# The last expert's contraction in two token passes in an attention, MLP and routed-expert kernel

## The chip, the cores and the metric

The kernel runs on one core of one Trainium2 chip, in one launch. The metric is device time in microseconds (us). The core has five engines: TensorE (PE, with its weight loads shown apart as PEld), VectorE (DVE), ScalarE (ACT), GpSimd (POOL) and SyncE (SP). Each has its own queue of instructions, and they meet through semaphores.

## What is computed

Three stages follow one another: attention over a window of 128 keys, a dense MLP, and eight experts to which 2304 tokens are routed, 288 to each. The change lies in the last stage alone, whose core is this (the routing, which fills `assigned`, is left out):

```python
def _moe2_ref(x, w_gate, w1, w2):
    N, D = x.shape                 # 2304, 512
    E = w_gate.shape[1]            # 8
    cap = N // E                   # 288
...
    out = np.zeros((N, D), dtype=np.float32)
    for e in range(E):
        mask = assigned == e
        h = np.maximum(x[mask] @ w1[e], 0.0)
        out[mask] = h @ w2[e]
    return out.astype(np.float32)
```

`w1` is 512 x 1024 for each expert and `w2` is 1024 x 512. Every product of two float32 numbers is made of three products of the reduced type fp32r: both operands are split into a high part (`wh`, `hh`) and a low part (`wl`, `hl`), and wh x hh, wl x hh and wh x hl are summed in PSUM.

## The kernel before

In the expert stage all engines run in the order in which the code is written (`manual_schedule`), so the order around the change is the order of the Python loops from L1041 on.

For each expert, `expand_expert(e, f)` (L975) makes one of eight blocks of 128 hidden features for all 288 tokens: 12 matmuls, a relu on ACT into `hh`, the low part on DVE into `hl`. Then `contract_expert(e, d)` (L995) makes one of four blocks of 128 output features: 24 matmuls (8 hidden blocks f, three products each) into the PSUM bank `y`. The stationary operand of each is a 128 x 128 piece of `w2` (`wh_w` or `wl_w`), and the moving operand is `hh` or `hl`, 128 x 288. Consecutive matmuls have different stationary operands, so each has its weight load of 128 columns. ACT then copies the bank to `yt[:, d, :]` (L1008). The banks with the tag `s` are two.

The results are feature-major and have to be written as rows of tokens. `output_transpose(e, g, d)` (L1012) transposes one block of 128 features by 96 tokens (g is one of three groups of 96 tokens, GR in the code) on PE into the bank `yo`; its moving operand is a 128 x 128 identity and its stationary one a 128 x 96 piece of `yt`. `output(e, g)` (L1017) copies the four blocks to `ys` (on ACT or on DVE) and lets POOL scatter its 96 rows to their places in the output by an indirect DMA (L1025), behind a tiny memset (L1024).

For experts 0 to 6 the transposes and outputs stand between the expansions of the expert after. For the last one nothing follows: three transposes, one of each group, stand behind each of the output blocks 1, 2 and 3 (they are those of the block before), and the three transposes of block 3 and all three outputs stand behind the last matmul (L1055 to L1060).

Of the kernel before, what the change touches and what calls it, by code (L numbers as in the profile page):

```python
# [14 lines left out]
AF = mybir.ActivationFunctionType  # L15
# [9 lines left out]
NE = 8  # L25
CAP = N // NE
# [47 lines left out]
G = 3  # L74
GR = CAP // G
# [51 lines left out]
def tile_attn_moe_moe2(ctx: ExitStack, tc: tile.TileContext, q_in, k_in, v, w_in, w_out, w_gate, w1, w2, consts, out):  # L127
    nc = tc.nc
    V, A, T, GP = nc.vector, nc.scalar, nc.tensor, nc.gpsimd
# [9 lines left out]
    def bank(tag, name, bufs=None):  # L139
        kw = {} if bufs is None else dict(bufs=bufs)  # L140
        return ps.tile([P, 512], F32, tag=tag, name=name, **kw)
# [109 lines left out]
    def gather(e):  # L251
        for g in range(G):
            xg[e, g] = xpool.tile([GR, DM], F32, tag="xg", name=f"xg_{e}_{g}", bufs=3)
            col = e * G + g
            src, at = (x2_dram[:, :], row) if e else (x2_dram[:N, :], idx)
            gathers[e, g] = GP.indirect_dma_start(
                out=xg[e, g], out_offset=None, in_=src,
                in_offset=bass.IndirectOffsetOnAxis(ap=at[:, col:col + 1], axis=0))
# [44 lines left out]
    with ExitStack() as actx:  # L303
# [279 lines left out]
        if True:  # L583
# [36 lines left out]
            s = 0  # L620
# [10 lines left out]
            while s <= max(NQ, late_end) or items or pending or tail:  # L631
# [5 lines left out]
                k = conv_at.get(s)  # L637
# [50 lines left out]
                for _ in range(2):  # L688
                    if s > gate_end and tail:
                        if staged and (len(tail) > 7 or len(items) <= len(tail)):  # L690
                            pool, lst, _, name = tail.pop(0)
# [257 lines left out]
    def gathered(e, g):  # L949
        if g == 0:  # L950
            expert_input(e)
        x = xg.pop((e, g))
        pt = bank("vlt"[g], f"xt_{e}_{g}", **({} if g == 2 else dict(bufs=1)))[:, :4 * GR].rearrange("p (d t) -> p d t", d=4)
        for d in range(4):
            T.transpose(pt[:, d, :], x[:, d * P:(d + 1) * P], ident[:GR, :GR])
        xh, xl = (t[:, :, g * GR:(g + 1) * GR] for t in xe[e])
        A.activation(xh, pt, AF.Copy)
        V.tensor_tensor(out=xl, in0=pt, in1=xh.bitcast(F32), op=ALU.subtract)
# [3 lines left out]
    def weights(n):  # L962

        nonlocal n_stage, n_split
        for _ in range(n):
            if n_split < 8 * NE:
                ready_w[n_split] = weight_tiles(ring[n_split % len(ring)](), f"w_{n_split}")
                split_weight(staged_w.pop(n_split), *ready_w[n_split], V)
                n_split += 1
            while n_stage < min(n_split + C_STAGES, 8 * NE):  # L970
                staged_w[n_stage] = stage(weight_src(n_stage), f"w_{n_stage}", epool,
                                          gathers[0, W_G] if n_stage == W_STAGED else None)
                n_stage += 1

    def expand_expert(e, f):  # L975
        if f == 0:
            hidden[e] = tuple(epool.tile([P, 8, CAP], F32R, tag=f"h{x}", name=f"h{x}_{e}", bufs=1)
                              for x in "hl")
        wh, wl = (t.rearrange("p (d f) -> p d f", d=4)[:, :, f % 2 * P:f % 2 * P + P]
                  for t in ready_w[8 * e + f // 2])  # L980
        (xh, xl), (hh, hl) = xe[e], hidden[e]
        hp = bank("h", f"m1_{e}_{f}")[:, :CAP]
        k = 0
        for w, x in ((wh, xh), (wl, xh), (wh, xl)):
            for d in range(4):
                T.matmul(hp, w[:, d, :], x[:, d, :], start=(k == 0), stop=(k == 11))  # L986
                k += 1
        A.activation(hh[:, f, :], hp, AF.Relu)
        V.scalar_tensor_tensor(out=hl[:, f, :], in0=hp, scalar=0.0, in1=hh[:, f, :].bitcast(F32),
                               op0=ALU.max, op1=ALU.subtract)  # L990
        weights(C_E0[f] if e == 0 else C_F[f])

    hidden, yt = {}, {}

    def contract_expert(e, d):  # L995
        if d == 0:
            yt[e] = epool.tile([P, 4, CAP], F32, tag="yt", name=f"yt_{e}", bufs=1)
        hh, hl = hidden[e]
        yp = bank("s", f"y_{e}_{d}")[:, :CAP]
        k = 0  # L1000
        for f in range(8):
            c = f % 2 * DM + d * P
            wh, wl = (t[:, c:c + P] for t in ready_w[8 * e + 4 + f // 2])
            for w, x in ((wh, hh), (wl, hh), (wh, hl)):
                T.matmul(yp, w, x[:, f, :], start=(k == 0), stop=(k == 23))  # L1005
                k += 1
        weights(1)
        A.activation(yt[e][:, d, :], yp, AF.Copy)  # L1008

    yo = {}  # L1010

    def output_transpose(e, g, d):  # L1012
        if d == 0:
            yo[g] = bank("ttv"[g], f"yo_{e}_{g}", **(dict(bufs=1) if g == 2 else {}))[:GR]
        T.transpose(yo[g][:, d * P:(d + 1) * P], yt[e][:, d, g * GR:(g + 1) * GR], ident)

    def output(e, g, on_act=True):  # L1017
        ys = epool.tile([GR, DM], F32, tag="ys", name=f"ys_{e}_{g}", bufs=3)
        if on_act:
            A.activation(ys, yo.pop(g), AF.Copy)  # L1020
        else:
            V.tensor_copy(ys, yo.pop(g))
        col = e * G + g
        GP.memset(spacer, 0.0)  # L1024
        sc = GP.indirect_dma_start(  # L1025
            out=out[:, :], out_offset=bass.IndirectOffsetOnAxis(ap=idx[:, col:col + 1], axis=0),
            in_=ys, in_offset=None)
        for other in scatters:
            tc.declare_no_dep(sc.ins, other.ins, reason="a token has one place")
        scatters.append(sc)  # L1030
# [10 lines left out]
    for e in range(NE):  # L1041
        for f in range(8):
            expand_expert(e, f)
            if f in (1, 2, 3) and e:
                for d in range(4):
                    output_transpose(e - 1, f - 1, d)
                output(e - 1, f - 1)
            if f == 4 and e + 1 < NE:
                gather(e + 1)
        for d in range(4):  # L1050
            contract_expert(e, d)
            if e + 1 < NE:
                if d < G:
                    gathered(e + 1, d)
            elif d:  # L1055
                for g in range(G):
                    output_transpose(e, g, d - 1)
    for g in range(G):
        output_transpose(NE - 1, g, 3)
        output(NE - 1, g, g != 1)  # L1060
    by_hand.close()


# [44 lines left out]
```

## Time and profile before

| | us |
|---|---|
| median of 3 runs | 915.43 |
| lowest and highest of them | 915.07 and 917.85 |
| the profiled execution, its own time | 917.14 |
| its span in the profile | 915.2 |

| engine | busy us | share of the span | instructions |
|---|---|---|---|
| PE | 841.4 | 92% | 7590 |
| PEld | 734.6 | 80% | 7590 |
| DVE | 521.9 | 57% | 1315 |
| ACT | 387.0 | 42% | 841 |
| POOL | 108.9 | 12% | 104 |

The profile is of one execution; its span is the time from its first to its last instruction. A matmul's duration in it is longer than its share of the engine's time, since matmuls are pipelined: what counts is the time from one start to the next, called a step below. A row that merges several instructions gives the time from the first's start to the last's end.

### The profile page before, as it was taken

How to read it: one execution, taken by the hardware profiler on the slowest of the kernel's cores; microseconds unless marked ns; L12 is line 12 of the kernel's file. 1: busy time of each engine (PE TensorE's matmuls, PEld its weight loads, DVE VectorE, ACT ScalarE, POOL GpSimd, SP SyncE). 2: the span in 40 equal slices, each digit the busy share in tenths (PEclk: the TensorE clock that was granted, in tenths of full speed). 3: DMA queues.
4: the chain of work that ended last, by engine and by line, in shares of the span. 5: the costliest groups of instructions: out<-in, count | busy, mean ns of one | idle time of the engine just before them, and what ended most of it. 6: DMA issues, size and time to landing. Idle time of an engine off the chain costs nothing.

```text
span 915.2 us, 18665 instructions
## 1 busy us (share of the span) xinstructions
PE 841.4 (92%) x7590; PEld 734.6 (80%) x7590; DVE 521.9 (57%) x1315; ACT 387.0 (42%) x841; POOL 108.9 (12%) x104
## 2 busy tenths in 40 slices
PE   2358698999999799999999999998999999999996
PEld 2347697999999688887677776776889999999995
DVE  3696856666654433247678777676235554555540
ACT  4454557566655544232212121211125555555551
POOL 1144411121110000000000000000020221122211
PEclk9998799999999899999999999998999999999998
DMA  9544666577546986585323324221425665676630
GB/s 275 158 157 141 217 179 190 159 226 235 163 127 171 286 227 159 147 246 148 141 93 107 119 77 133 85 98 52 130 104 187 191 183 168 190 226 201 187 122 27
DMA packets 103637, 147.19 MB, mean 161 GB/s; under 512 B 6144, under 2 KB 74368, under 8 KB 101504
## 3 DMA queue, kind: packets, MB, share of 16 engines
q1 hardware_dynamic: 100480, 136.56, 49.9%
q0 software_dynamic: 3072, 9.44, 3.1%
q8 instruction: 60, 0.98, 0.4%
q14 instruction: 25, 0.20, 0.1%
HBM read 113.21 MB, written 32.77 MB: 160 GB/s over the span
## 4 chain that ended last, share of the span: by engine, by line
PE 79%; DVE 9%; ACT 3%; issue 3%; DMA 3%; POOL 2%; SPq 0%; POOLq 0%; ACTq 0%; DVEq 0%
PE po L223 22%; PE h L505 20%; PE m L986 10%; PE y L1005 10%; PE xv L480 3%; PE cnt L806 3%; PE pt L463 2%; DMA raw<-in_w_in_dram 2%; PE lg L532 2%; PE s L421 2%; DVE dt L357 1%; DVE dt L356 1%; DVE dt L358 1%; PE wtp L384 1%; ACT pr L439 1%
## 5 line engine op out<-in xcount | busy, mean ns | idle before, releaser
L223 PE MATMUL po<-wh_out,gol 128*128 128x512 f32 x272 | 112.5, 414 | 4.7 <-DVE gol L191 4.6
L518 DVE TENSOR_TENSOR gb<-h,th 128x512 f32<-128x512 f32 x72 | 49.7, 691 | 109.1 <-ACT th L514 108.5
L223 PE MATMUL po<-wh_out,goh 128*128 128x512 f32 x272 | 110.9, 408 | 0.0
L223 PE MATMUL po<-wl_out,goh 128*128 128x512 f32 x272 | 110.6, 407 | 0.0
L505 PE MATMUL h<-xh,wh_in 128*128 128x256 f32 x576 | 96.0, 290 | 4.6 <-DVE gb L518 4.6
L505 PE MATMUL h<-xh,wl_in 128*128 128x256 f32 x576 | 91.9, 283 | 1.1 <-POOL wl_in L372 1.1
L505 PE MATMUL h<-xl,wh_in 128*128 128x256 f32 x576 | 90.9, 280 | 0.0
L183 ACT ACTIVATE goh<-gin 128x1024 fp32r<-128x1024 f32 x34 | 36.0, 1060 | 129.0 <-DMA gin<-g_dram 113.4
L160 DVE TENSOR_TENSOR wl_w<-st_w,wh_w 128x1024 fp32r<-128x1024 f32 x60 | 72.9, 1224 | 25.8 <-ACT wh_w L159 25.8
L505 PEld LDWEIGHTS h<-xh,wh_in 128*128 128x128 f32 x576 | 79.4, 194 | 9.7 <-DVE gb L518 4.8
L514 ACT ACTIVATE th<-h 128x512 f32<-128x512 f32 x72 | 42.7, 593 | 94.1 <-PE h L505 93.8
L505 PEld LDWEIGHTS h<-xh,wl_in 128*128 128x128 f32 x576 | 79.2, 194 | 1.3 <-POOL wl_in L372 1.3
L505 PEld LDWEIGHTS h<-xl,wh_in 128*128 128x128 f32 x576 | 78.3, 192 | 0.0
L439 ACT ACTIVATE pr<-neg,nm 128x192 f32<-128x192 f32 (+2 forms) x144 | 61.2, 426 | 40.4 <-DVE nm L436 40.3
L1005 PE MATMUL y<-hh,wh_w 128*128 128x288 f32 x256 | 77.4, 302 | 0.0
L1005 PE MATMUL y<-hh,wl_w 128*128 128x288 f32 x256 | 75.6, 295 | 0.0
L1005 PE MATMUL y<-hl,wh_w 128*128 128x288 f32 x256 | 75.5, 295 | 0.0
L223 PEld LDWEIGHTS po<-wh_out,gol 128*128 128x128 f32 x272 | 51.7, 190 | 15.9 <-DVE gol L191 6.3
L159 ACT ACTIVATE wh_w<-st_w 128x1024 fp32r<-128x1024 f32 x60 | 62.5, 1053 | 2.0 <-DMA st_w<-in_w_dram 2.0
L421 PE MATMUL s<-k,q 64*64 64x192 f32 (+2 forms) x576 | 35.7, 358 | 28.1 <-DVE nm L436 9.9
L368 POOL TENSOR_TENSOR dt<-dt,de 128x1024 f32<-128x1024 f32 x16 | 37.9, 2366 | 187.3 <-DVE de L366 115.6
L223 PEld LDWEIGHTS po<-wl_out,goh 128*128 128x128 f32 x272 | 51.7, 190 | 10.3 <-issue 0.2
(220 smaller groups left out, 1589.4 us busy)
## 6 DMA issues: line engine op xcount, KB each, us to landing
st_w<-in_w_dram SPq DMA_DIRECT2D x64, 512.0 KB, 3.9
g_dram<-gb SPq DMA_DIRECT2D x72, 256.0 KB, 4.5
gin<-g_dram SPq DMA_DIRECT2D x34, 512.0 KB, 3.8
gr<-g_dram SPq DMA_DIRECT2D x48, 256.0 KB, 5.8
v<-in_v_dram SPq DMA_DIRECT2D x28, 384.0 KB, 5.5
raw<-in_w_in_dram SPq DMA_DIRECT2D x8, 1024.0 KB, 5.4
raw<-in_w_out_dram SPq DMA_DIRECT2D x8, 1024.0 KB, 6.1
x_dram<-xo SPq DMA_DIRECT2D x17, 256.0 KB, 2.1
```

Of the source, the lines that this page charges most:

```text
L159: A.activation(wh, st, AF.Copy)
L160: lo_engine.tensor_tensor(out=wl, in0=st, in1=wh.bitcast(F32), op=ALU.subtract)
L183: A.activation(wh, st, AF.Copy)
L223: T.matmul(po, g, w, start=(k == 0), stop=(k == 47))
L368: (V if k in ADD_V else GP).tensor_tensor(out=t, in0=t, in1=e, op=ALU.add)
L421: T.matmul(s[a][x * Q:x * Q + Q, hf, :], qt[rows, c, t0:t0 + Q], ktile[b][rows, c, (m + 1) * Q - nk:(m + 1) * Q], start=True, stop=True, t ...
L439: A.activation(pr[:, i, :nk], neg[:, a, :nk], AF.Exp, scale=-1.0, bias=nm[:, i:i + 1], accum_out=sm[:, i:i + 1])
L505: T.matmul(hp[:, j, :], w[:, d, j * P:(j + 1) * P], x[:, d, :], start=(k == 0), stop=(k == 11))
L514: A.activation(th, hp, AF.Copy, scale=0.01)
L518: V.tensor_tensor(out=gbs[c][:, o:o + 2, :], in0=hp, in1=th, op=ALU.max)
L986: T.matmul(hp, w[:, d, :], x[:, d, :], start=(k == 0), stop=(k == 11))
L1005: T.matmul(yp, w, x[:, f, :], start=(k == 0), stop=(k == 23))
```

## The change

The last expert's contraction is made twice over the same weights: first for tokens 0 to 191 (groups 0 and 1, four banks of 128 x 192), then for tokens 192 to 287 (group 2, four banks of 128 x 96). The transposes and outputs of groups 0 and 1 stand behind the second block of the second pass. Behind the last matmul there are the last two transposes and the output of group 2, which DVE now copies. Experts 0 to 6 are left as they were.

```diff
-    def contract_expert(e, d):
-        if d == 0:
+    def contract_expert(e, d, t0=0, t1=CAP):
+        if d == 0 and t0 == 0:
             yt[e] = epool.tile([P, 4, CAP], F32, tag="yt", name=f"yt_{e}", bufs=1)
         hh, hl = hidden[e]
-        yp = bank("s", f"y_{e}_{d}")[:, :CAP]
+        yp = bank("s", f"y_{e}_{d}_{t0}")[:, :t1 - t0]
...
-                T.matmul(yp, w, x[:, f, :], start=(k == 0), stop=(k == 23))
+                T.matmul(yp, w, x[:, f, t0:t1], start=(k == 0), stop=(k == 23))
                 k += 1
         weights(1)
-        A.activation(yt[e][:, d, :], yp, AF.Copy)
+        A.activation(yt[e][:, d, t0:t1], yp, AF.Copy)
...
-        for d in range(4):
-            contract_expert(e, d)
-            if e + 1 < NE:
+        if e + 1 < NE:
+            for d in range(4):
+                contract_expert(e, d)
                 if d < G:
                     gathered(e + 1, d)
-            elif d:
-                for g in range(G):
-                    output_transpose(e, g, d - 1)
-    for g in range(G):
-        output_transpose(NE - 1, g, 3)
-        output(NE - 1, g, g != 1)
+
+    e = NE - 1
+    for d in range(4):
+        contract_expert(e, d, 0, 2 * GR)
+    for d in range(4):
+        contract_expert(e, d, 2 * GR, CAP)
+        for g in range(2) if d == 1 else ():
+            for x in range(4):
+                output_transpose(e, g, x)
+        for g in range(2) if d == 1 else ():
+            output(e, g)
+        if d:
+            output_transpose(e, 2, d - 1)
+    output_transpose(e, 2, 3)
+    output(e, 2, False)
```

The order of PE at the program's end, before (`y_3` is the bank of output block 3, `yo_0` to `yo_2` the transposes' banks of the three token groups):

```order
L1005 MATMUL y_3_10750<-hh_10501,wl_w_10629 128x288
L1005 MATMUL y_3_10750<-hl_10502,wh_w_10628 128x288
L1015 MATMUL yo_0_10715<-cst,yt_10662 96x128
L1015 MATMUL yo_1_10717<-cst,yt_10662 96x128
L1015 MATMUL yo_2_10719<-cst,yt_10662 96x128
L1015 MATMUL yo_0_10715<-cst,yt_10662 96x128
L1015 MATMUL yo_1_10717<-cst,yt_10662 96x128
L1015 MATMUL yo_2_10719<-cst,yt_10662 96x128
L1104 UNCONDITIONAL_BRANCH
```

Six transposes stand behind the last matmul, of which the last three need the last block's copy.

The order of PE in the second pass of the change (`y_1_192` is output block 1 of tokens 192 to 287):

```order
L1005 MATMUL y_1_192_10793<-hl_10502,wh_w_10628 128x96
L1015 MATMUL yo_0_10819<-cst,yt_10662 96x128 x4
L1015 MATMUL yo_1_10824<-cst,yt_10662 96x128 x4
L1015 MATMUL yo_2_10837<-cst,yt_10662 96x128
L1005 MATMUL y_2_192_10839<-hh_10501,wh_w_10494 128x96
...
L1015 MATMUL yo_2_10837<-cst,yt_10662 96x128
L1005 MATMUL y_3_192_10866<-hh_10501,wh_w_10494 128x96
...
L1005 MATMUL y_3_192_10866<-hl_10502,wh_w_10628 128x96
L1015 MATMUL yo_2_10837<-cst,yt_10662 96x128 x2
L1113 UNCONDITIONAL_BRANCH
```

Nine transposes now stand between the second and the third of the four 96-token blocks, one behind the third, and two behind the last.

The order of ACT at the program's end, before and then in the change (`yt` are the copies of the banks `y`, `ys` those of the banks `yo`):

```order
L1008 ACTIVATE yt_10662<-y_2_10721 128x288
L1008 ACTIVATE yt_10662<-y_3_10750 128x288
L1020 ACTIVATE ys_0_10780<-yo_0_10715 96x512
L1020 ACTIVATE ys_2_10790<-yo_2_10719 96x512
L1104 UNCONDITIONAL_BRANCH
```

```order
L1008 ACTIVATE yt_10662<-y_3_0_10741 128x192
L1008 ACTIVATE yt_10662<-y_0_192_10767 128x96
L1008 ACTIVATE yt_10662<-y_1_192_10793 128x96
L1020 ACTIVATE ys_0_10829<-yo_0_10819 96x512
L1020 ACTIVATE ys_1_10833<-yo_1_10824 96x512
L1008 ACTIVATE yt_10662<-y_2_192_10839 128x96
L1008 ACTIVATE yt_10662<-y_3_192_10866 128x96
L1113 UNCONDITIONAL_BRANCH
```

The copies of groups 0 and 1 now stand ahead of the last two copies of `yt`, and POOL's three scatters follow in the order 0, 1, 2 as before.

## Rows read from the trace of the kernel before

**Rows 1.** The profile's page, its first line.

```profile
span 915.2 us, 18665 instructions
```

**Rows 2.** Stretches near the end: us, busy time of each engine, PEclk, DMA share, GB/s.

```profile
900.00:905.00 5.00, 5.00 (x40) 5.00 (x39) 0.00 (x0) 0.41 (x1) 0.00 (x0) 1.00 0.00 0
905.00:910.00 5.00, 1.20 (x9) 0.69 (x7) 0.69 (x1) 1.49 (x3) 2.51 (x5) 0.96 0.20 56
```

**Rows 3.** Timeline of the end: start us, us, engine line op, [idle before <-releaser].

```profile
905.05 0.29 PE L1005 MATMUL y<-hl,wh_w 128*128 128x288 f32 x1
...
905.38 0.41 ACT L1008 ACTIVATE yt<-y 128x288 f32<-128x288 f32 x1 [3.10 <-PE y L1005]
...
905.84 0.53 PE L1015 MATMUL yo<-cst,yt 128*96 128x128 f32 x3 [0.17 <-ACT yt L1008]
906.19 1.08 ACT L1020 ACTIVATE ys<-yo 96x512 f32<-96x512 f32 x2 [0.41 <-PE yo L1015]
906.30 0.69 DVE L1022 COPY ys<-yo 96x512 f32<-96x512 f32 x1 [13.45 <-PE yo L1015]
907.06 0.92 POOL L1025 DMA_INDIRECT out_dram<-ys,idx  x1 [18.45 <-ACT ys L1020]
...
908.28 0.92 POOL L1025 DMA_INDIRECT out_dram<-ys,idx  x1 [0.22 <-issue]
...
909.51 0.92 POOL L1025 DMA_INDIRECT out_dram<-ys,idx  x1 [0.21 <-issue]
```

**Rows 4.** Timeline of the last expert's contraction, its first matmul and its blocks 1 and 2.

```profile
891.75 0.29 PE L1005 MATMUL y<-hh,wh_w 128*128 128x288 f32 x1
...
898.01 0.29 PE L1005 MATMUL y<-hl,wh_w 128*128 128x288 f32 x1
...
898.36 0.19 PEld L1005 LDWEIGHTS y<-hh,wh_w 128*128 128x128 f32 x1
898.39 0.38 PE L1005 MATMUL y<-hh,wh_w 128*128 128x288 f32 x1
898.47 0.19 PEld L1005 LDWEIGHTS y<-hh,wl_w 128*128 128x128 f32 x1
898.60 0.30 PE L1005 MATMUL y<-hh,wl_w 128*128 128x288 f32 x1
...
901.53 0.29 PE L1005 MATMUL y<-hl,wh_w 128*128 128x288 f32 x1
```

**Rows 5.** Timeline: matmuls of fp32r operands of other widths, 256 and 512.

```profile
400.35 0.62 PE L505 MATMUL h<-xh,wh_in 128*128 128x256 f32 x4
...
678.29 0.39 PE L223 MATMUL po<-wl_out,goh 128*128 128x512 f32 x1
...
678.51 0.39 PE L223 MATMUL po<-wh_out,gol 128*128 128x512 f32 x1
```

**Rows 6.** Timeline: narrow matmuls and transposes of plain float32 operands.

```profile
678.74 2.81 PE L266 MATMUL xt<-cst,xg 96*128 96x96 f32 x24
...
309.66 0.88 PE L421 MATMUL s<-k,q 64*64 64x192 f32 x16
...
867.06 0.49 PE L955 MATMUL xt<-cst,xg 96*128 96x96 f32 x4
```

**Rows 7.** Single instructions of two lines: duration ns min/median/max, first and last start.

```profile
L266 PE MATMUL xt<-cst,xg x24: 246/275/275, 678.7 to 681.3; 96*128 96x96 f32 x24
...
L955 PE MATMUL xt<-cst,xg x4: 244/246/247, 867.1 to 867.3; 96*128 96x96 f32 x4
```

**Rows 8.** Timeline: a copy from PSUM by ACT of another width.

```profile
867.63 0.48 ACT L957 ACTIVATE eh<-xt 128x384 fp32r<-128x384 f32 x1
```

**Rows 9.** Timeline: PE behind a long wait in the attention stage.

```profile
78.94 1.22 PE L505 MATMUL h<-xh,wh_in 128*128 128x256 f32 x4 [4.57 <-DVE gb L518]
...
82.52 1.05 PE L505 MATMUL h<-xh,wl_in 128*128 128x256 f32 x4
```

**Rows 10.** The stretch of those matmuls, columns as in rows 2.

```profile
77.00:84.00 7.00, 5.06 (x25) 5.06 (x26) 3.12 (x4) 2.59 (x4) 3.03 (x2) 0.53 0.34 75
```

## The prediction, made before the changed kernel was run

> **What bounds the kernel now.** I read three views: the stretches near the end, then the timeline of the end, then the timeline of the last expert's contraction with the narrow matmuls elsewhere. The span is 915.2 us [rows 1]. From 900 to 905 us both PE and its weight loads are busy without a gap, at a granted clock of 1.00, and no other engine has more than one short copy to do; from 905 us on PE is nearly idle [rows 2]. So the last expert's contraction is bound by PE, and behind it stands a tail in which PE does almost nothing. The change shortens the tail and lengthens what PE has to do; each microsecond of either goes straight into the span, as nothing else runs there.
>
> The contraction goes from the start of its first matmul, 891.75 us, to that of its last, 905.05 us [rows 3, 4]: 13.30 us, with 96 matmuls and nine transposes in it. Its step is 0.133 us: 22 steps from 898.60 to 901.53 [rows 4]. Three transposes between two blocks lengthen two steps to 0.59 us (898.01 to 898.60), so a transpose costs (0.59 - 2 x 0.133) / 3 = 0.108 us.
>
> The tail goes from 905.05 to 915.2 us, 10.15 us. In order [rows 3]: 0.33 us until ACT starts the last copy of `yt`, 0.41 the copy, 0.05 until the transposes, 0.35 until the first copy to `ys`, 0.54 that copy (two take 1.08), 0.33 until POOL's first scatter starts at 907.06, two rounds of POOL until its third starts at 909.51 (2.45), and 5.69 from there to the end, in which the rows are written and the program closes.
>
> **What the change takes away.** Of the three scatters behind the last matmul one remains: 2.45 us less. The last copy of `yt` has 96 columns, not 288. A copy of 384 columns takes 0.48 us and one of 288 takes 0.41 [rows 3, 8], 0.07 for 96 columns, so it takes 0.27: 0.14 less. The copy to `ys` is DVE's at 0.69 in place of ACT's at 0.54: 0.15 more. The new tail is 0.33 + 0.27 + 0.05 + 0.35 + 0.69 + 0.33 + 5.69 = 7.71 us, **2.44 us less**. The transpose ahead of the last one hides behind the last copy of `yt`. The copies and scatters of groups 0 and 1 cost nothing: they run beside the last two blocks, some 5 us of PE work, on ACT and POOL, which have nothing else there [rows 2]. On ACT the copy of block 2 of the second pass is queued behind the two copies to `ys`; it has a whole block of matmuls to start in before anyone needs it. If that cover were gone, the two copies would add 1.08 us. Memset and DMA instructions are as many as before, and SP's queue is as it was.
>
> **What it adds.** 96 matmuls of 288 columns become 96 of 192 and 96 of 96. The columns that stream through PE are as many as before; the weight loads are twice as many. So all hangs on what a step costs when the moving operand is narrow. The trace has no fp32r matmul below 256 columns, and I bound the step from rows near it.
>
> - From below: if only the columns counted, a step would shrink with the width, to 0.089 and 0.044 us.
> - The weight load. Behind three transposes the loads of the contraction are late, and the next one starts 0.11 us after the one before (898.36, 898.47) while the matmuls still wait for them [rows 4]. A weight load of 128 columns thus holds the loading path for 0.11 us. Today it hides behind a step of 0.133.
> - The nearest narrow matmuls: 24 of plain float32 with 96 columns and loads of 128 columns take 2.81 us, the last one's own 0.275 included [rows 6, 7]: (2.81 - 0.275) / 23 = 0.110 us a step, the same figure.
> - From above: sixteen float32 matmuls of 192 columns, four at a time in quarters of the array, take 0.88 us [rows 6], at most 0.22 us for each four.
>
> I take 0.111 us for both widths, since the two rows with a load of this size agree on it: a step is then the load's time, whatever the width. The Trainium skill (TensorE: Matmul & The Clock Gate, section LDWEIGHTS) speaks against the change in the same way: a load's time comes from its columns alone, 107 ns for 128, and by it the whole sum would be 0.8 us smaller. Rows 4 and 6 agree with that rule for products; the transposes of L955 do not, which also load 128 columns and step at (0.49 - 0.246) / 3 = 0.081 us [rows 6, 7].
>
> The contraction then has 191 steps of 0.111 = 21.20 us. Ten transposes stand inside it (nine and one; the last two are behind it). At 0.108 they make 1.08 us; before, part of that was caught up again, because the loads were quicker than the steps, and now there is nothing to catch up with. Together 22.28 us against 13.30: **8.98 us more**. The first block waits for nothing new: its last products need the low part of hidden block 7, and they come 21 steps of 0.111 after its start, 2.3 us in place of 2.8, by when ACT and DVE have long finished one block of 288 columns.
>
> **Sum.** + 8.98 - 2.44 = + 6.54 us. The sum is against the span of 915.2; the execution's own time, 917.14, lies 1.9 us above it, and the median of the runs is 915.43. Nothing outside the span changes, so I add to the median: **922.0 us**. With steps of 0.107 to 0.114, transposes at 0.07 to 0.125 and half a microsecond for the median, this case reaches from 920.3 to 923.4.
>
> **Rivals.**
>
> 1. *The columns bind, not the loads* (ends not slower). If two loads could run at once, steps would be 0.089 and 0.044 us. 95.5 x 0.133 + 1.08 - 13.30 = + 0.5, less 2.44: - 1.9 us, 913.5; with the transposes hidden as well, 912.4. It decides where the two steps together fall below 0.153 us (95.5 x 0.153 + 1.08 - 13.30 = 2.4), 0.077 for each. For it: the transposes at 0.081. Against it: 0.11 between loads of this very kind. Chance 0.05.
> 2. *Narrow matmuls come at a rate of their own.* From rows that would be the transposes' 0.081 us for 96 columns [rows 6, 7] and, where the columns count again, 0.089 for 192: 95.5 x 0.170 + 1.08 - 13.30 - 2.44 = + 1.6, 917.0. The Trainium skill (same page, section Back-to-back issue gap) has such a rule: pairs of load and matmul at 81 ns for 128 columns and 131 for 512. At 512 columns this trace shows 0.22 us (678.29 to 678.51) [rows 5], so the rule does not hold for these operands. Chance 0.03.
> 3. *Narrow fp32r is no faster than plain float32.* Then 192 columns cost up to 0.22 us and 96 columns 0.110: the first pass adds 96 x 0.109 = 10.4, 932.4. No row shows fp32r below 256 columns, so it can't be excluded; the 96-column row of plain float32, no slower than my step, speaks against a harsh penalty. Chance 0.05.
> 4. *PE's clock falls.* In the second pass the array streams for less than half of each step. Behind a wait of 4.57 us the same four matmuls took 1.05 us in place of 0.62 [rows 5, 9], in a stretch at a granted clock of 0.53 [rows 10], which is mostly the lower of the two levels, 1.2 of 2.4 GHz. At 69% to 100% more for the second pass: 7.4 to 10.7 us more, 929 to 933. Against it: PE had stood idle there, while both passes feed it without a pause. Chance 0.04.
> 5. *The first two scatters don't leave early*, for a copy or a queue that I have missed. Then the gain is gone and 9.0 us remain: 924.4. The order of ACT and POOL in the change speaks against it. Chance 0.03.
>
> **How the numbers follow.** The forecast has 0.80. The range takes it in with rival 5, from 920.3 to 924.5, and leaves out rivals 1 to 4, 0.17. What can be told from no change is about 0.3%, 2.7 us. Slower: the forecast and rivals 3, 4 and 5, 0.92. Rivals 1 and 2 end within 0.3%, but for the low end of rival 1: same 0.07, faster 0.01.
>
> **What would show it.** Right: the groups of the contraction's matmuls with 192 and with 96 columns both at steps of about 0.11 us with PEld busy throughout; some 22.3 us from the first to the last of them; one scatter behind the last matmul and about 7.7 us from its start to the end; PEclk 1.00 until the tail. Wrong: a step of 96 columns clearly below 0.11 (rivals 1 and 2), a step of 192 columns well above it (rival 3), both doubled late (rival 4), or scatters at the end as before (rival 5).

## The result, and the profile after

| | before | changed |
|---|---|---|
| median of 4 runs, us | 915.25 | 929.28 |
| lowest and highest, us | 914.45, 917.85 | 926.94, 930.12 |
| span of the profiled execution, us | 915.2 | 928.1 |

The ratio is 1.0144, with a 95% interval from 1.0116 to 1.0173: 14 us slower, where 6.5 were forecast, and above the stated range.

The page of the changed kernel, its first line and the granted clock in 40 slices of 23.2 us:

```profile
span 928.1 us, 18861 instructions
...
PEclk9998799999999899999999999998999999999995
```

The last slice is at half. Two stretches of the second pass show where (us, busy time of PE, PEld, DVE, ACT and POOL, PEclk, DMA share, GB/s):

```profile
901.50:905.20 3.70, 3.70 (x36) 3.70 (x35) 0.00 (x0) 0.58 (x2) 0.00 (x0) 1.00 0.00 0
905.20:920.50 15.30, 15.30 (x76) 15.22 (x75) 0.00 (x0) 1.69 (x4) 2.01 (x4) 0.50 0.09 26
```

PE has no gap in either, and its weight loads almost none (15.22 of 15.3 us in the second). The first has 36 matmuls in 3.7 us, the second 76, its transposes among them, in 15.3, at the lower level of 1.2 GHz. The timeline of the changed kernel, from the first matmul of the contraction on, answers to [rows 3, 4]:

```profile
890.85 0.25 PE L1005 MATMUL y<-hh,wh_w 128*128 128x192 f32 x1
...
901.44 0.27 PE L1005 MATMUL y<-hl,wh_w 128*128 128x192 f32 x1
901.55 0.23 PE L1005 MATMUL y<-hh,wh_w 128*128 128x96 f32 x1
901.62 0.28 PE L1005 MATMUL y<-hh,wl_w 128*128 128x96 f32 x1
...
905.19 0.33 PE L1005 MATMUL y<-hh,wh_w 128*128 128x96 f32 x1
905.32 0.41 PE L1005 MATMUL y<-hh,wl_w 128*128 128x96 f32 x1
905.53 0.41 PE L1005 MATMUL y<-hl,wh_w 128*128 128x96 f32 x1
...
910.33 0.92 POOL L1025 DMA_INDIRECT out_dram<-ys,idx  x1 [22.61 <-ACT ys L1020]
911.55 0.92 POOL L1025 DMA_INDIRECT out_dram<-ys,idx  x1 [0.22 <-issue]
...
920.24 0.41 PE L1005 MATMUL y<-hl,wh_w 128*128 128x96 f32 x1
920.69 0.25 ACT L1008 ACTIVATE yt<-y 128x96 f32<-128x96 f32 x1 [4.97 <-PE y L1005]
921.48 0.69 DVE L1022 COPY ys<-yo 96x512 f32<-96x512 f32 x1 [29.52 <-PE yo L1015]
922.44 0.92 POOL L1025 DMA_INDIRECT out_dram<-ys,idx  x1 [9.88 <-DVE ys L1022]
```

What the reader is to see:

- The first pass keeps a step of (901.44 - 890.85) / 95 = 0.111 us with 192 columns. The second starts at the same step: (905.19 - 901.55) / 33 = 0.110 with 96 columns. The forecast's central price held for both.
- At 905.2 us, 3.7 us into the second pass and ahead of its first transpose, the step goes to 0.213 and stays there to the end.
- The contraction takes 920.24 - 890.85 = 29.4 us where 22.3 were forecast. 61 steps of matmuls and 10 of transposes fall into the slow part: 71 x (0.213 - 0.111) = 7.2 us. That is the whole difference.
- Two scatters leave at 910 and 911 us, beside the matmuls, and one is left for the tail, which takes 928.1 - 920.24 = 7.9 us where 7.7 were forecast and 10.15 were there before.

So 16.1 us were added (29.4 - 13.3) and 2.3 taken off the tail (10.15 - 7.9). The profiled span grew by 12.9 and not 13.8, because the stages ahead happened to end 0.9 us sooner (890.85 against 891.75). The profiles below differ by some microseconds in that (the last contraction starts between 886.4 and 893.1 us where it is shown), so their timelines are read from the contraction's first matmul on.

### The profile page after: what moved, and what is told of

Same layout as the page of the kernel before. It is cut to its first block, busy times and chain, and to the rows that moved or that the text cites. A ratio compares the mean times of both kernels' runs of the same rounds, so it can differ in the third digit from the quotient of the medians.

```text
span 928.1 us, 18861 instructions
## 1 busy us (share of the span) xinstructions
PE 856.2 (92%) x7686; PEld 749.1 (81%) x7686; DVE 522.2 (56%) x1315; ACT 388.1 (42%) x845; POOL 108.9 (12%) x104
## 4 chain that ended last, share of the span: by engine, by line
PE 75%; DVE 9%; issue 5%; ACT 4%; DMA 3%; POOL 1%; SPq 1%; POOLq 0%; ACTq 0%; DVEq 0%
PE po L223 22%; PE h L505 18%; PE m L986 10%; PE y L1005 10%; PE cnt L806 3%; PE xv L480 2%; PE pt L463 2%; DMA raw<-in_w_in_dram 2%; PE lg L532 2%; PE s L421 2%; DMA st_out<-wo_dram 1%; DVE dt L357 1%; DVE dt L356 1%; DVE dt L358 1%; ACT pr L439 1%
## 5 line engine op out<-in xcount | busy, mean ns | idle before, releaser
L1005 PE MATMUL y<-hh,wh_w 128*128 128x288 f32 (+2 forms) x288 | 88.1, 306 | 0.0
L1005 PE MATMUL y<-hh,wl_w 128*128 128x288 f32 (+2 forms) x288 | 86.6, 301 | 0.0
L1005 PE MATMUL y<-hl,wh_w 128*128 128x288 f32 (+2 forms) x288 | 86.5, 300 | 0.0
L463 PE MATMUL pt<-cst,pr 128*96 128x128 f32 (+2 forms) x256 | 41.0, 307 | 21.5 <-DVE pr L453 16.9
```

Source lines behind the costliest of these rows:

```text
L463: T.transpose(pt[:kn, a, kb, :], pr[:, 2 * hf + a, kb * kn:kb * kn + kn], ident)
L1005: T.matmul(yp, w, x[:, f, t0:t1], start=(k == 0), stop=(k == 23))
```

## The experiments

The changed kernel's trace shows that the clock fell and where, not what let it fall. The theory was the narrow stream: loads follow one another without a gap, but 96 columns stream in each step. Rivals were the doubled weight loads themselves, the time that PE had already been bound by them, and the quiet of the other engines at the program's end.

**A second pass as wide as the first.**

```diff
-                T.matmul(yp, w, x[:, f, t0:t1], start=(k == 0), stop=(k == 23))
+                T.matmul(yp, w, x[:, f, s0:t1], start=(k == 0), stop=(k == 23))
...
-        contract_expert(e, d, 2 * GR, CAP)
+        contract_expert(e, d, 2 * GR, CAP, GR)
...
```

> The second pass streams 192 columns (tokens 96 to 287) and copies only its last 96; weight loads, their number and their order are those of the changed kernel. Theory (it was the narrow stream of 96 columns that let the clock fall): PEclk 1.00 up to the tail, both passes at steps of 0.111 us, about 22.3 us from the contraction's first to its last matmul, 6.5 us above the kernel before (921 to 923). Rival (it is the doubled weight loads, or a long stretch bound by them): the clock falls in the second pass as in the changed kernel, and the time stays at 926 to 930.

Measured: 922.95 us (918.15 to 925.4), ratio 1.0076 (1.0048 to 1.0105), 7.8 us above the kernel before (915.18 in the same session). Stretches of its two passes and its tail, and its timeline:

```profile
890.60:901.20 10.60, 10.60 (x97) 10.60 (x97) 0.46 (x1) 1.41 (x4) 0.00 (x0) 1.00 0.01 2
901.20:912.90 11.70, 11.70 (x107) 11.70 (x107) 0.00 (x0) 2.17 (x6) 2.02 (x4) 1.00 0.11 34
912.90:920.60 7.70, 0.72 (x5) 0.32 (x4) 0.69 (x1) 0.25 (x1) 0.92 (x1) 0.68 0.09 26
```

```profile
890.56 0.25 PE L1006 MATMUL y<-hh,wh_w 128*128 128x192 f32 x1
...
912.93 0.27 PE L1006 MATMUL y<-hl,wh_w 128*128 128x192 f32 x1
...
914.86 0.92 POOL L1026 DMA_INDIRECT out_dram<-ys,idx  x1 [4.44 <-DVE ys L1023]
```

Both passes stay at 1.00. The contraction takes 912.93 - 890.56 = 22.4 us and the tail 920.6 - 912.93 = 7.7, together 30.0 against 23.45 before: 6.6 us more, the forecast's sum. As many weight loads, in the same order, do not lower the clock. Streaming twice the columns that are needed costs nothing, since a step is the load's time either way, and it saves some 6 us.

**The same with the outputs at the end.**

```diff
-        for g in range(2) if d == 1 else ():
-            for x in range(4):
-                output_transpose(e, g, x)
-        for g in range(2) if d == 1 else ():
-            output(e, g)
-        if d:
-            output_transpose(e, 2, d - 1)
-    output_transpose(e, 2, 3)
-    output(e, 2, False)
+        for g in range(G) if d else ():
+            output_transpose(e, g, d - 1)
+    for g in range(G):
+        output_transpose(e, g, 3)
+        output(e, g, g != 1)
```

> As e1_wide, but the transposes and the three outputs stand as in the kernel before: three transposes behind blocks 1 to 3, and all three outputs behind the last matmul. Theory: the early outputs are worth the two rounds of POOL, 2.4 us, so the time is 2.2 to 2.6 us above e1_wide, about 8.9 above the kernel before (924). Rival (the early outputs are worth nothing, or cost something in the pass): the same as e1_wide, or less.

Measured: 924.0 us (922.13 to 928.97), ratio 1.0109 (1.0061 to 1.0157). The medians differ by 1.1 us, less than the runs scatter, so the times alone do not decide. The timeline of its end does:

```profile
888.46 0.25 PE L1006 MATMUL y<-hh,wh_w 128*128 128x192 f32 x1
...
910.38 0.27 PE L1006 MATMUL y<-hl,wh_w 128*128 128x192 f32 x1
...
912.05 0.92 POOL L1026 DMA_INDIRECT out_dram<-ys,idx  x1 [26.72 <-ACT ys L1021]
...
913.27 0.92 POOL L1026 DMA_INDIRECT out_dram<-ys,idx  x1 [0.21 <-issue]
...
914.49 0.92 POOL L1026 DMA_INDIRECT out_dram<-ys,idx  x1 [0.22 <-issue]
```

With a span of 920.2 its tail is 9.8 us against 7.7 with early outputs: 2.1 us, two rounds of POOL (914.49 - 912.05 = 2.44) less the 0.3 us by which its first scatter starts sooner behind the last matmul (912.05 - 910.38 against 914.86 - 912.93). The contraction is 0.45 us shorter, with nine transposes in it and not ten, so the early outputs gain some 1.7 us in all, less than the 2.2 to 2.6 that were expected here. That is what the change was able to win.

**The passes exchanged.**

```diff
-        contract_expert(e, d, 0, 2 * GR)
+        contract_expert(e, d, 0, GR)
...
-        contract_expert(e, d, 2 * GR, CAP)
+        contract_expert(e, d, GR, CAP)
...
```

> The passes change places: tokens 0 to 95 first (96 columns), then tokens 96 to 287 (192 columns), with one early output and two late ones. Theory: the clock falls within the first pass, 3 to 7 us after its start, and comes back in the second; 926 to 930. Rival (the time that PE has been bound by weight loads decides): full clock through all of the first pass, as the changed kernel kept it for 14 us from the start of its passes, and a fall only in the second, if at all; 923 to 927.

Measured: 930.68 us (927.9 to 931.87), ratio 1.0168 (1.0127 to 1.0208), just above the expected 926 to 930. Stretches of its two passes:

```profile
886.70:891.20 4.50, 4.50 (x43) 4.50 (x41) 0.50 (x2) 0.66 (x2) 0.00 (x0) 1.00 0.00 0
891.20:903.00 11.80, 11.80 (x59) 11.80 (x57) 0.00 (x0) 0.50 (x2) 0.00 (x0) 0.50 0.00 1
903.00:908.40 5.40, 5.40 (x27) 5.40 (x28) 0.00 (x0) 0.25 (x1) 0.00 (x0) 0.51 0.00 0
908.40:917.00 8.60, 8.60 (x79) 8.60 (x79) 0.00 (x0) 1.59 (x4) 1.01 (x2) 1.00 0.08 23
```

The clock falls 4.5 us into the 96-column pass, which is now the first, and comes back 5.4 us into the 192-column pass. The time spent at load-bound steps before is thus not what decides, and the wide stream brings the clock back while the loads go on as before.

**Two passes in the middle of the program.**

```diff
...
+        for d in range(4) if e == 3 else ():
+            contract_expert(e, d, 0, 2 * GR)
         for d in range(4):
-            contract_expert(e, d)
+            if e == 3:
+                contract_expert(e, d, 2 * GR, CAP)
+            else:
+                contract_expert(e, d)
```

> The kernel before, with expert 3's contraction in two passes (192 columns, then 96) and its outputs where they were; the last expert is in one pass. Beside this contraction DVE, ACT and the DMA queues work on the next expert's weights. Theory: the clock falls in the pass of 96 columns and comes back in the next expert's expansion; 8.5 us for the steps and 3 to 8 for the clock, 927 to 932. Rival (the clock fell because everything but PE was quiet at the program's end): PEclk stays 1.00, 923 to 925.

Measured: 925.25 us (922.25 to 928.24), ratio 1.0106 (1.0057 to 1.0154). The 96-column pass of expert 3:

```profile
789.80:801.50 11.70, 11.70 (x110) 11.70 (x110) 6.41 (x8) 6.34 (x11) 0.00 (x0) 1.00 0.70 220
```

PEclk stays at 1.00: the theory as it stood fell here. Two things differ from the program's end. The other engines are busy (DVE 6.4 us of 11.7, DMA share 0.70), and the four transposes of the next expert's input stand behind each of the first three blocks of 24 matmuls. The next three runs take them apart.

**The middle again, without transposes in the narrow pass.** They move behind the blocks of the 192-column pass:

```diff
         for d in range(4) if e == 3 else ():
             contract_expert(e, d, 0, 2 * GR)
+            if d < G:
+                gathered(e + 1, d)
...
-                if d < G:
+                if d < G and e != 3:
                     gathered(e + 1, d)
```

> As e4_mid, but the transposes of the next expert's input stand behind the blocks of the first pass, so that the pass of 96 columns has none in it; DVE, ACT and the DMA queues are as busy beside it as in e4_mid. Theory (96-column matmuls alone let the clock fall; in e4_mid four transposes behind each block of 24 kept it): the clock falls 3 to 7 us into the pass of 96 columns and comes back in the next expansion, 928 to 932. Rival (busy neighbours kept it in e4_mid): PEclk 1.00 and steps of 0.11 us throughout, the time of e4_mid, 924 to 926.

Measured: 932.04 us (928.39 to 932.09), ratio 1.0162 (1.013 to 1.0195), 6.8 us above the run before it. Its stretches in the 96-column pass:

```profile
791.70:797.00 5.30, 5.30 (x51) 5.30 (x49) 2.67 (x3) 2.47 (x4) 0.00 (x0) 1.00 0.67 210
797.00:807.30 10.30, 10.30 (x51) 10.30 (x50) 2.51 (x3) 2.39 (x4) 0.00 (x0) 0.50 0.46 145
```

The clock falls 5.3 us into the pass. The copies and subtractions that belong to the transposes moved with them, so the neighbours were a little less busy before the fall than in the run before (DVE 2.67 of 5.3 us against 6.41 of 11.7, ACT 2.47 against 6.34). Neighbours that are about half busy did not keep the clock.

**The changed kernel with its transposes spread.** Four behind block 0, five behind block 1, four behind block 2 of the second pass; three of these are made twice:

```diff
-        for g in range(2) if d == 1 else ():
-            for x in range(4):
-                output_transpose(e, g, x)
+        for x in range(4) if d < 2 else ():
+            output_transpose(e, d, x)
...
+        if d == 2:
+            spare = bank("l", "spare", bufs=1)[:GR]
+            for x in range(3):
+                T.transpose(spare[:, x * P:(x + 1) * P], yt[e][:, x, :GR], ident)
```

> The changed kernel with its transposes spread over the pass of 96 columns: four behind block 0, five behind block 1, four behind block 2 (three of these are made twice, into a spare bank). DVE, ACT and the DMA queues are as quiet as in the changed kernel. Theory (transposes between the blocks keep the clock): PEclk 1.00 up to the tail, 22.6 us from the contraction's first to its last matmul, 921 to 924. Rival (quiet neighbours): the clock falls as in the changed kernel, 927 to 931.

Measured: 921.56 us (918.6 to 925.11), ratio 1.0074 (1.0046 to 1.0102). Its second pass, and its timeline:

```profile
897.10:909.00 11.90, 11.90 (x111) 11.90 (x109) 0.00 (x0) 2.05 (x6) 2.01 (x4) 1.00 0.11 33
```

```profile
886.41 0.25 PE L1005 MATMUL y<-hh,wh_w 128*128 128x192 f32 x1
...
908.97 0.28 PE L1005 MATMUL y<-hl,wh_w 128*128 128x96 f32 x1
```

PEclk is 1.00 at 96 columns, with quiet neighbours, in the profiled execution, which is the quickest of the five; all five are below the changed kernel's lowest, 926.94. The contraction takes 22.56 us and with the tail, to 916.7, it is 30.3 us: 6.8 more than the 23.45 before. The change as forecast exists, then; it needs transposes behind each of the first three narrow blocks, not nine behind one.

**Busy neighbours alone.** Eight copies on ACT and eight subtractions on DVE beside the changed kernel's second pass, PE's order left as it was:

```diff
+        for x in range(2) if d < 3 else ():
+            V.tensor_tensor(out=ready_w[8 * e][1], in0=ready_w[8 * e][0].bitcast(F32),
+                            in1=ready_w[8 * e + 1][0].bitcast(F32), op=ALU.subtract)
+            A.activation(ready_w[8 * e + 2][1], ready_w[8 * e + 2][0].bitcast(F32), AF.Copy)
```

(two more of each stand ahead of the second pass)

> The changed kernel with eight copies of 1024 columns on ACT and eight subtractions of 1024 columns on DVE added beside the second pass, on tiles that nothing reads any more; PE's order is that of the changed kernel. Theory (what PE itself streams decides): the clock falls in the second pass as in the changed kernel, 926 to 931. Rival (busy neighbours keep it): PEclk 1.00 up to the tail, 921 to 924.

Measured: 928.03 us (922.44 to 929.9), ratio 1.0134 (1.0107 to 1.0161). Its stretches:

```profile
886.40:897.10 10.70, 10.70 (x98) 10.70 (x97) 9.80 (x10) 1.41 (x4) 0.00 (x0) 1.00 0.01 2
897.10:900.70 3.60, 3.60 (x35) 3.60 (x34) 0.39 (x1) 3.06 (x5) 0.00 (x0) 0.99 0.00 0
900.70:907.50 6.80, 6.80 (x35) 6.72 (x34) 0.00 (x0) 4.68 (x7) 0.14 (x1) 0.50 0.00 0
907.50:912.00 4.50, 4.50 (x43) 4.50 (x42) 0.00 (x0) 2.33 (x4) 1.89 (x4) 1.00 0.30 87
```

The nine transposes behind block 1 of its second pass:

```profile
904.09 2.14 PE L1015 MATMUL yo<-cst,yt 128*96 128x128 f32 x9
```

DVE waited for nothing and did its part beside the first pass, so this tests ACT alone: busy for 3.06 of 3.6 us, it did not keep the clock, which fell 3.6 us into the pass. The clock came back at 907.5, some 3.4 us after the first of these nine. In the changed kernel it did not come back after the same nine. Why not is left open; in both they follow matmuls at the lower level. The profiled execution, 922.44, is also the quickest of the five by 5 us; the other four, 927.42 to 929.9, lie where the changed kernel's do, and no profile shows whether the clock came back in them.

**The operands exchanged.** For each token group, hidden features stationary and 512 columns of `w2` streaming, so rows of tokens come out at once and nothing is transposed:

```diff
...
+    for g in range(G):
+        yo[g] = bank("sst"[g], f"yr_{e}_{g}")[:GR]
+        k = 0
+        for f in range(8):
+            wh, wl = (t[:, f % 2 * DM:f % 2 * DM + DM] for t in ready_w[8 * e + 4 + f // 2])
+            for w, x in ((wh, hh), (wl, hh), (wh, hl)):
+                T.matmul(yo[g], x[:, f, g * GR:(g + 1) * GR], w, start=(k == 0), stop=(k == 23))
+                k += 1
+        output(e, g, g != 2)
```

> The last expert's contraction with its operands exchanged: for each group of 96 tokens the hidden features are the stationary operand (96 columns to load) and a 512-column row of the output weights streams, so 24 matmuls a group make 96 rows of tokens at once; no copy to yt and no transposes for this expert, and the outputs of groups 0 and 1 leave early. Theory: a wide stream keeps the clock and hides the load: 72 steps of 0.225 us = 16.2 us in place of 13.3, and a tail of 0.33 + 0.69 + 0.33 + 5.69 = 7.0 us in place of 10.15, together 0.4 us under the kernel before (914.9, no difference that can be measured). Rival (steps of 0.225 do not hold with a load of 96 columns, or the early copies hold PE up): 917 or more.

Measured: 915.36 us (912.61 to 918.62, 12 runs) against 916.33, ratio 0.9996 (0.9973 to 1.002): no difference. Its timeline:

```profile
893.12 0.39 PE L1064 MATMUL yr<-wh_w,hh 128*96 128x512 f32 x1
...
909.58 0.40 PE L1064 MATMUL yr<-wh_w,hl 128*96 128x512 f32 x1
910.01 0.69 DVE L1022 COPY ys<-yr 96x512 f32<-96x512 f32 x1 [15.79 <-PE yr L1064]
910.98 0.92 POOL L1025 DMA_INDIRECT out_dram<-ys,idx  x1 [4.60 <-DVE ys L1022]
```

71 steps take 16.46 us, 0.232 each, and the tail is 916.7 - 909.58 = 7.1. Together 23.6 us against 23.45. It is 6.4 us quicker than the two wide passes at full clock (30.0) and gives the early outputs without doubling the loads, yet what the tail gains (3.0) the longer contraction takes (3.2).

## Why the prediction was wrong

The direction held, and so did the two sums, of the contraction and of the tail, wherever the clock stayed at its upper level. It did not stay there in the changed kernel. Point by point:

- *A step is the weight load's time, whatever the width, 0.111 us.* Held: 0.111 at 192 columns, 0.110 at 96, while the clock was at its upper level. Rival 1 (columns bind), rival 2 (a rate of their own) and rival 3 (narrow fp32r as slow as plain float32) fell with it. The load's 107 ns in the Trainium skill (TensorE: Matmul & The Clock Gate, section LDWEIGHTS) stands 4% below what was measured.
- *The contraction takes 22.28 us.* 22.4 with the wide second pass and 22.56 with three transposes added, both at full clock; 29.4 in the changed kernel. (The upper end of this case, 923.4, is a slip: 191 x 0.114 + 10 x 0.125 - 13.30 - 2.44, half a microsecond and 915.43 make 923.2. Nothing hangs on it.)
- *The tail takes 7.71 us, 2.44 less.* 7.7 at full clock and 7.9 in the changed kernel. Rival 5 (the scatters do not leave early) fell: they start at 910 and 911 us.
- *The clock holds; rival 4 has a chance of 0.04.* **This step failed**, with its reason: "PE had stood idle there, while both passes feed it without a pause". The passes did feed it without a pause, and the clock fell all the same, 3.7 us into the second. Rival 4 had named the mechanism, and 929.28 lies in its 929 to 933. Its price per step was right, 69% to 100% more (measured: 0.213 for 0.111, 92% more); but it charged all of the second pass, and only 71 steps were slow, so the 7.2 us lost lie just below its 7.4 to 10.7.

The mistake was to take the one fall that the prediction shows, behind a wait of 4.57 us, for the only kind (the four matmuls directly behind that wait took 1.22 us; the 1.05 is from later in the same stretch [rows 9]). The trace of before has five falls ahead of its tail. Four came while PE stood still, but one, at 155.3 us, came while it worked:

```profile
155.00:159.00 4.00, 4.00 (x55) 3.25 (x55) 2.56 (x11) 2.46 (x9) 0.00 (x0) 0.57 0.71 259
```

```profile
154.40 0.66 PE L384 MATMUL wtp<-cst,dt 128*128 128x128 f32 x4 [1.14 <-ACT wg L404]
154.99 1.36 PE L421 MATMUL s<-k,q 64*64 64x192 f32 x16
156.28 1.97 PE L480 MATMUL xv<-pts,v 96*64 96x64 f32 x32
```

PE had started again 0.9 us earlier, behind a wait of 1.14 us, and the clock then stayed low for some 3 us in which PE, with small matmuls, had no gap. Waits stand shortly ahead of it, so it is not a clean case, but it spoke against the prediction's reason and was left out. Beyond it the trace has no long stretch of narrow matmuls with loads of 128 columns: the 24 of [rows 6] were over in 2.81 us, and the earliest fall in the runs above came 3.6 us into the narrow pass. That was an absence of evidence, and it deserved more than 0.04. That the array streams for less than half of each step was named in rival 4 and then set aside.

The Trainium skill (TensorE: Matmul & The Clock Gate, section Why this matters for your kernels) speaks of gaps in which PE idles as what loses the clock. This case adds that a stream without any gap can lose it. The Trainium skill says of transposes (same page, section Part 4: PE-mode transpose) that they don't count as PE-busy in the same way. No run here has transposes alone, so that sentence is not tested; what the runs show is that the pass with four of them behind each of its first three blocks kept the clock and the same pass without them lost it (789.8 to 801.5 and 797.0 to 807.3 us above).

What is shown, in one profiled execution of each kernel and in line with their times: moving the transposes out of the narrow pass beside busy neighbours lost the clock, and spreading them in it beside quiet ones kept it; and a wider stream at the same loads kept it and brought it back. What is not shown is by which quantity the chip tells these apart, nor why nine transposes in one place were followed by the upper level once and not the other time.

## What to carry to other kernels

Splitting a matmul's moving operand doubles the weight loads, and once the columns take less time than the load, each half costs a full load: here 192 steps of 0.111 us stood in the place of 96 of 0.133, to take some 2.4 us off the tail. A PE row that is busy without a gap is not yet a PE at full clock: when a change makes the stream much narrower than the load, as the 96 columns did here, give the low clock a real chance and look for wider work to stream or for transposes to place between. If the first outputs must leave early, exchange the operands rather than split the narrow one, and count first whether there is a gain left: here there was none.

## What the runs showed of the hardware that was not expected

- PE without a gap, at 96-column fp32r matmuls, went from a granted clock of 1.00 to 0.50 after 3.6 to 5.3 us in four kernels, and steps went from 0.111 to 0.213 us.
- 192 columns at the same step of 0.111 us kept 1.00 for 22 us, and where they followed a narrow pass at 0.50, 1.00 came back 5.4 us after they began. Padding the narrow stream with columns that nobody reads made the changed kernel about 6 us faster (929.28 and 922.95).
- With four transposes behind each of the first three blocks of 24 narrow matmuls, 1.00 held for the whole pass of 11.7 us.
- At a granted clock of 0.50 a step that a weight load sets is doubled with the rest, at 96 columns (0.213 us) and, where the passes were exchanged, at 192 (27 matmuls in 5.4 us).
